# Output columns ordered for 512-byte stores, GpSimd's additions moved to VectorE, in an attention and gated-FFN kernel

## The chip, the core and the metric

The kernel runs on one core of one Trainium2 chip. The metric is the device time of one execution in microseconds; a kernel's time is the median of its runs.

## The reference, cut to what matters

```python
# x: 8 batches, 8 heads, 512 tokens, 64 wide; state: 32 rows a head; all float32
scores  = x @ state.T / 8;  xread = softmax(scores) @ state
scores2 = state @ x.T / 8;  sread = softmax(scores2) @ x
x = concat([xread, sread]) as 4352 rows of 512
x = ((x @ w1) * (x @ w2)) @ w3 @ w_out                      # 512 -> 1024 -> 1024 -> 512
return (sigmoid(x @ w_gate) * (x @ w_val)) @ w_out2         # 512 -> 1536 -> 512
```

The weights of both feed-forward parts arrive as 64-bit floats and are turned into 32-bit ones in the kernel.

## The kernel before

Every product is made of three passes of TensorE over a high and a low part of each operand (`split`: ScalarE copies the high part, a subtraction makes the low part).

**First half.** It does the attention and the first feed-forward part, one batch after another, with attention folded in between the products. Each batch is a loop over eight column blocks (`j`) and then four output blocks (`d`): twelve slots, in which other work is placed. The result `y` goes to DRAM (`y_d`), already transposed. In the same slots the weights of the second part are prepared: `prep_group` makes 18 groups of four steps (two loads with conversion, `sums`, `last`). A group holds the seven combinations of a 2 x 2 blocked weight that Winograd's form of Strassen's algorithm needs: three blocks as they are, and four sums (`sm`). All seven are split into the staging tile `wst`, the arithmetic on GpSimd, and one store on GpSimd's queue brings them to `w_d` or `wo_d`.

**Second half.** The 34 blocks of 128 token rows go in five pairs of 8, 8, 6, 6 and 6 blocks. One operand of a product is half a pair, 512 or 384 columns. Each pair takes three passes over 512 of the 1536 hidden columns. A pass is `gate_val` twice (14 steps each) and `down` (14 steps); a step is six products into one PSUM bank. `down` of a pass runs behind the first three steps of the next pass's `gate_val`. Its results are added up over the passes in eight SBUF tiles `acc[d, cc]` (`d`: 128 output columns, `cc`: half of the pair). Results that go into two tiles are copied to SBUF by ScalarE (`sv`) and added by GpSimd (`also`); the others are added by VectorE from PSUM (`more`).

The order of ScalarE, VectorE, GpSimd and SyncE is written out by hand: `later(k, cost, fn)` puts `fn` at the beginning of the k-th step from now, `begin` advances a model clock, and `fill` places parts of the next pair's `y` (`next_tokens`) where the model sees VectorE free. An operation of n columns counts n/720 us in it.

Weights stream through SyncE's queue (`Stream`): `wt`, one tile of 256 KB a step of `gate_val`, 19 tiles; `wo`, one of 512 KB for two steps of `down`, 4 tiles. A new load is issued behind the step that used the tile and waits for it in the queue. At the end of a pair, `store` transposes one `acc` tile in 32 x 32 blocks on VectorE into a tile `sv` (three of them, shared with `also`) and issues 16 or 12 stores of 32 partitions on the same queue, each 128 descriptors of 128 bytes:

```python
            for i, fn in enumerate(done):
                later(2 + 2 * i, n / 720, fn)
```

The last pair does the same behind the last product (`tail`). In the rows, the products of `gate_val` are L1386 and those of `down` L1543; the weight loads are L1246, the output stores L1480, their transposes L1466, `more` L1490, `also` L1494, subtractions of the second half (`minus`) L1109 and of the first (`split`) L163, and all copies of ScalarE L158.

Of the kernel before, what the change touches and what calls it, by code (L numbers as in the profile page):

```python
# [117 lines left out]
def tile_state_attention__then__gated_ffns(  # L118
# [19 lines left out]
    nc = tc.nc  # L138
# [124 lines left out]
    with tc.manual_schedule(engines={mybir.EngineType.PE}):  # L263
# [781 lines left out]
        def prep_group(dst, srcs, by_rows):  # L1045
# [6 lines left out]

            def sums():
                t = ab["t"] = p2["wst"].tile([P, 7, 2, 256], F32R, name="wst")
                sm = ab["sm"] = p2["wst"].tile([P, 4, 256], F32, name="sm")
                halves = [[v[:, i * 256 : (i + 1) * 256] for i in range(2)] for v in m]
                (a11, a12), (a21, a22) = halves if by_rows else zip(*halves)
                for o, x0, x1, op in (
                    (0, a21, a22, ALU.add),
                    (1, sm[:, 0], a11, ALU.subtract),  # L1060
                    (2, a11, a21, ALU.subtract),
                    (3, a12, sm[:, 1], ALU.subtract),
                ):
                    nc.gpsimd.tensor_tensor(out=sm[:, o], in0=x0, in1=x1, op=op)
                if by_rows:
                    split(
                        t[:, 0:2, 0], t[:, 0:2, 1], m[0].rearrange("p (k f) -> p k f", k=2),
                        sub=nc.gpsimd,
                    )
                else:  # L1070
                    split(t[:, 0, 0], t[:, 0, 1], a11, sub=nc.gpsimd)
                    split(t[:, 1, 0], t[:, 1, 1], a12, sub=nc.gpsimd)
                split(t[:, 2, 0], t[:, 2, 1], a22, sub=nc.gpsimd)

            def last():
                t = ab["t"]
                split(t[:, 3:7, 0], t[:, 3:7, 1], ab["sm"], sub=nc.gpsimd)
                nc.gpsimd.dma_start(out=dst, in_=t.rearrange("p o i f -> p (o i f)").bitcast(F32))
# [21 lines left out]
        def y_raw(c, kb, h, pool, w, queue=nc.sync):  # L1100
            n = blocks[c] * P // 2
            r = pool.tile([P, 2, w], F32, tag="raw", name="yf", bufs=3)
            queue.dma_start(
# [25 lines left out]
        for t, b in enumerate(order):  # L1129
# [124 lines left out]
        def next_tokens(c, at):  # L1254
# [9 lines left out]
            def get(kb, h, queue=nc.sync):  # L1264
                raw[kb, h] = y_raw(c, kb, h, c2, NB, queue)
                clock["load"] = landed[kb, h] = max(clock["load"], clock["us"] + 2.5) + 2.2

            def diffs(kb):
                (b11, b12), (b21, b22) = raw[kb, 0], raw[kb, 1]
                t[kb] = [c2.tile([P, NB], F32, tag="m", name="yt", bufs=3)[:, :n] for _ in range(3)]  # L1270
# [8 lines left out]
            def part(o, kb):  # L1279
                def fn():  # L1280
# [9 lines left out]
                    later(1, n / 720, lambda: (minus(y[1], v, y[0].bitcast(F32)), ready.add((c, o, kb))))  # L1290
                    if (o, kb) == (5, 0):
                        later(2, 0.0, lambda: get(1, 1, nc.scalar))
# [21 lines left out]
            out += [(at(9), False, lambda i=i: diff(1, i)) for i in range(4)]  # L1314
# [15 lines left out]
        def operand(s, jj):  # L1330
# [15 lines left out]
            later(1, n / 720, low)  # L1346
# [5 lines left out]
        def have(q, jj, cc, n):  # L1352

            cost = n / 720
# [18 lines left out]
        def gate_val(c, g, q, between):  # L1373
# [31 lines left out]
            def finish(a, jj, cc, o, what):  # L1405

                if a == 0:
# [6 lines left out]
                    vector(n / 720)  # L1414
# [225 lines left out]
```

## Time and profile before

| | |
|---|---|
| median of 3 runs | 1543.65 us (1542.5 to 1547.69) |
| the profiled execution | 1541.75 us, span 1540.0 us |
| granted clock of TensorE, mean | 0.937 of full speed |
| busy: TensorE, VectorE, ScalarE, GpSimd | 1318.2, 928.4, 661.6, 263.8 us |
| moved by DMA | 312.90 MB, 203 GB/s over the span |
| DMA packets under 512 bytes | 121552 of 240444 |

The span runs from the first to the last instruction; the time has 1.75 us more around it. Busy times of engines overlap, so they don't add up to the span.

### The profile page before, as it was taken

How to read it: one execution, taken by the hardware profiler on the slowest of the kernel's cores; microseconds unless marked ns; L12 is line 12 of the kernel's file. 1: busy time of each engine (PE TensorE's matmuls, PEld its weight loads, DVE VectorE, ACT ScalarE, POOL GpSimd, SP SyncE). 2: the span in 40 equal slices, each digit the busy share in tenths (PEclk: the TensorE clock that was granted, in tenths of full speed). 3: DMA queues.
4: the chain of work that ended last, by engine and by line, in shares of the span. 5: the costliest groups of instructions: out<-in, count | busy, mean ns of one | idle time of the engine just before them, and what ended most of it. 6: DMA issues, size and time to landing. Idle time of an engine off the chain costs nothing. (4 is left out here: it accounts for less than half of the span.)

```text
span 1540.0 us, 21873 instructions
## 1 busy us (share of the span) xinstructions
PE 1318.2 (86%) x7792; PEld 1120.7 (73%) x7792; DVE 928.4 (60%) x1532; ACT 661.6 (43%) x1274; POOL 263.8 (17%) x232
## 2 busy tenths in 40 slices
PE   8999999999999999999856999657996699876970
PEld 5587787777777798877745887557986699776970
DVE  5975766755777626577644569343683466753670
ACT  6964664665566534335212435131342243331330
POOL 0000452443354100030100032000210010100210
PEclk9999999999999999999978999887997899988995
DMA  8974776857866338676436776438874688548712
GB/s 300 336 211 151 230 262 240 277 218 272 296 224 234 143 115 311 199 228 200 128 87 196 203 215 181 116 85 278 262 221 126 191 274 259 163 111 265 235 49 34
DMA packets 240444, 312.90 MB, mean 203 GB/s; under 512 B 121552, under 2 KB 139472, under 8 KB 233424
## 3 DMA queue, kind: packets, MB, share of 16 engines
q1 hardware_dynamic: 229904, 263.54, 55.6%
q0 software_dynamic: 3168, 37.23, 6.4%
q10 hardware_dynamic: 7264, 10.75, 2.0%
q8 instruction: 62, 1.02, 0.3%
q14 instruction: 46, 0.38, 0.1%
HBM read 256.38 MB, written 55.05 MB: 202 GB/s over the span
## 5 line engine op out<-in xcount | busy, mean ns | idle before, releaser
L1386 PE MATMUL psA<-y,wt 128*128 128x384 f32 (+1 forms) x1440 | 311.4, 364 | 46.9 <-ACT u L158 45.1
L1543 PE MATMUL po<-ph,wo 128*128 128x384 f32 (+1 forms) x1260 | 265.6, 369 | 81.5 <-DMA wo<-wod 60.9
L1386 PEld LDWEIGHTS psA<-y,wt 128*128 128x128 f32 x1440 | 265.6, 193 | 74.9 <-ACT u L158 47.9
L1543 PEld LDWEIGHTS po<-ph,wo 128*128 128x128 f32 x1260 | 232.9, 195 | 111.8 <-issue 63.7
L158 ACT ACTIVATE u<-psA 128x384 f32<-128x384 f32 (+1 forms) x120 | 63.9, 532 | 300.0 <-PE psA L1386 265.8
L1494 POOL TENSOR_TENSOR acc<-sv,acc 128x384 f32<-128x384 f32 (+1 forms) x60 | 94.2, 1604 | 509.2 <-ACT sv L158 427.3
L1386 PE MATMUL psB<-y,wt 128*128 128x384 f32 (+1 forms) x720 | 163.1, 362 | 0.0
L1386 PEld LDWEIGHTS psB<-y,wt 128*128 128x128 f32 x720 | 133.2, 192 | 11.6
L1490 DVE TENSOR_TENSOR acc<-po,acc 128x384 f32<-128x384 f32 (+1 forms) x140 | 82.8, 601 | 91.5 <-PE po L1543 91.0
L225 PE MATMUL py<-u,wp 128*128 128x512 f32 (+1 forms) x576 | 133.0, 382 | 1.9 <-ACT u L158 1.1
L225 PE MATMUL pab<-aT,sw 128*128 128x512 f32 x448 | 124.0, 398 | 4.9 <-DVE asb L983 3.5
L225 PEld LDWEIGHTS py<-u,wp 128*128 128x128 f32 x576 | 102.9, 188 | 30.6 <-issue 7.5
L1386 PE MATMUL psC<-y,wt 128*128 128x384 f32 (+1 forms) x360 | 84.8, 372 | 26.1 <-DVE s L1419 26.1
L1109 DVE TENSOR_TENSOR ph<-p,ph 128x384 fp32r<-128x384 f32 (+1 forms) x120 | 96.0, 803 | 17.8 <-ACT ph L158 17.7
L1466 DVE STREAM_TRANSPOSE sv<-acc 128x384 f32<-128x384 f32 (+1 forms) x40 | 25.1, 628 | 128.9 <-DMA out<-sv 128.8
L225 PEld LDWEIGHTS pab<-aT,sw 128*128 128x128 f32 x448 | 82.6, 190 | 24.8 <-DVE asb L983 5.2
L163 DVE TENSOR_TENSOR u<-asb,u 128x512 fp32r<-128x512 f32 (+1 forms) x64 | 67.0, 1046 | 42.6 <-ACT u L158 42.3
L1386 PEld LDWEIGHTS psC<-y,wt 128*128 128x128 f32 x360 | 67.7, 197 | 34.3 <-DVE s L1419 28.6
L1415 ACT ACTIVATE p<-p 128x384 f32<-128x384 f32 (+1 forms) x90 | 50.7, 563 | 91.1 <-DVE p L1413 91.1
L158 ACT ACTIVATE ph<-t 128x384 fp32r<-128x384 f32 (+1 forms) x90 | 49.7, 563 | 75.2 <-DVE t L1109 74.1
L1413 DVE TENSOR_TENSOR p<-psB,u 128x384 f32<-128x384 f32 (+1 forms) x60 | 36.5, 609 | 73.0 <-ACT u L158 67.2
L158 ACT ACTIVATE ph<-p 128x384 fp32r<-128x384 f32 (+1 forms) x120 | 64.7, 561 | 28.6 <-DVE p L1422 28.5
(137 smaller groups left out, 1988.0 us busy)
## 6 DMA issues: line engine op xcount, KB each, us to landing
wt<-wd SPq DMA_DIRECT2D x420, 256.0 KB, 3.1
wo<-wod SPq DMA_DIRECT2D x105, 512.0 KB, 4.2
wq<-w12d SPq DMA_DIRECT2D x32, 1024.0 KB, 7.1
wd<-wst POOLq DMA_DIRECT2D x12, 1792.0 KB, 7.2
raw<-in_moe_w SPq DMA_DIRECT2D x32, 512.0 KB, 6.2
wod<-wst POOLq DMA_DIRECT2D x6, 1792.0 KB, 7.5
raw<-in_moe_w_out SPq DMA_DIRECT2D x20, 512.0 KB, 6.4
out<-sv SPq DMA_DIRECT2D x544, 16.0 KB, 1.5
```

Of the source, the lines that this page charges most:

```text
L158: return nc.scalar.activation(out=o, in_=i, func=AF.Copy)
L163: (sub or nc.vector).tensor_tensor(out=lo, in0=src, in1=hi.bitcast(F32), op=ALU.subtract)
L225: nc.tensor.matmul(o, w[i], xx[k], start=begin and n == 0 and i + k == 0, stop=False)
L1109: nc.vector.tensor_tensor(out=o, in0=x0, in1=x1, op=ALU.subtract)
L1386: nc.tensor.matmul(o, w[:, i, kb * P : (kb + 1) * P], xx[kb][h], start=start, stop=i == 1 and kb == 1, skip_group_check=True,)
L1413: nc.vector.tensor_tensor(out=t, in0=o, in1=kept[a, what], op=ALU.add)
L1415: later(2, 0.0, lambda: nc.scalar.activation(out=t, in_=t, func=AF.Sigmoid))
L1466: nc.vector.transpose(out=t, in_=acc[d, cc])
L1490: nc.vector.tensor_tensor(out=acc[d, cc], in0=o, in1=acc[d, cc], op=ALU.add)
L1494: nc.gpsimd.tensor_tensor(out=acc[d, cc], in0=v, in1=acc[d, cc], op=ALU.add)
L1543: nc.tensor.matmul(o, w[:, jj, i, d * P : (d + 1) * P], x[h], start=k in (1, 6, 2) and jj == 0 and i + h == 0, stop=jj == 1 and i == 1, sk ...
```

## The change

The columns of `w_out2` are taken in another order when its blocks are formed, so that a 32 x 32 transpose of the four `acc` tiles of one 128-row block leaves 128 neighbouring output columns beside each other. `store` then handles one block of 128 rows with all 512 columns: four transposes and four stores whose descriptors are 512 bytes. They are placed every three steps. For the last pair `last_store` turns a block with four transposes on TensorE into PSUM, ScalarE or VectorE copies it, and one store of 128 rows goes out, in turn on SyncE's and ScalarE's queue. The additions that GpSimd made in `also`, in the copy of `acc` and in `prep_group` are VectorE's; `wst` becomes two tiles of three and four blocks, each with a store of its own. The `y` of the next pair is loaded by four loads at once, its differences are formed as soon as they have landed, and it has 4 and 6 tiles (`raw`, `yt`) instead of 3 and 3; `wt` has 16 tiles instead of 19. The preparation uses twelve slots of a batch instead of eleven. The model counts n/840 instead of n/720 (these lines and a dropped argument `queue` are left out below).

```diff
+            def shape(v):
+                return v if by_rows else v.rearrange("p (c i d) -> p c i d", c=2, i=4)
             def sums():
-                t = ab["t"] = p2["wst"].tile([P, 7, 2, 256], F32R, name="wst")
                 sm = ab["sm"] = p2["wst"].tile([P, 4, 256], F32, name="sm")
-                halves = [[v[:, i * 256 : (i + 1) * 256] for i in range(2)] for v in m]
-                (a11, a12), (a21, a22) = halves if by_rows else zip(*halves)
+                t = p2["wst"].tile([P, 3, 2, 256], F32R, name="wsta")
+                if by_rows:
+                    (a11, a12), (a21, a22) = [[v[:, i * 256 : (i + 1) * 256] for i in range(2)] for v in m]
+                else:
+                    (a11, a21), (a12, a22) = [
+                        [
+                            v.rearrange("p (i c d) -> p c i d", i=4, c=4)[:, 2 * i : 2 * i + 2]
+                            for i in range(2)
+                        ]
+                        for v in m
+                    ]
+                s1, s2, s3, s4 = (shape(sm[:, o]) for o in range(4))
                 for o, x0, x1, op in (
-                    (0, a21, a22, ALU.add),
-                    (1, sm[:, 0], a11, ALU.subtract),
-                    (2, a11, a21, ALU.subtract),
-                    (3, a12, sm[:, 1], ALU.subtract),
+                    (s1, a21, a22, ALU.add),
+                    (s2, s1, a11, ALU.subtract),
+                    (s3, a11, a21, ALU.subtract),
+                    (s4, a12, s2, ALU.subtract),
                 ):
-                    nc.gpsimd.tensor_tensor(out=sm[:, o], in0=x0, in1=x1, op=op)
-                if by_rows:
-                    split(
-                        t[:, 0:2, 0], t[:, 0:2, 1], m[0].rearrange("p (k f) -> p k f", k=2),
-                        sub=nc.gpsimd,
-                    )
-                else:
-                    split(t[:, 0, 0], t[:, 0, 1], a11, sub=nc.gpsimd)
-                    split(t[:, 1, 0], t[:, 1, 1], a12, sub=nc.gpsimd)
-                split(t[:, 2, 0], t[:, 2, 1], a22, sub=nc.gpsimd)
+                    nc.vector.tensor_tensor(out=o, in0=x0, in1=x1, op=op)
+                for o, v in enumerate((a11, a12, a22)):
+                    split(shape(t[:, o, 0]), shape(t[:, o, 1]), v)
+                store(0, t)
             def last():
-                t = ab["t"]
-                split(t[:, 3:7, 0], t[:, 3:7, 1], ab["sm"], sub=nc.gpsimd)
-                nc.gpsimd.dma_start(out=dst, in_=t.rearrange("p o i f -> p (o i f)").bitcast(F32))
+                t = p2["wst"].tile([P, 4, 2, 256], F32R, name="wstb")
+                for o in range(0, 4, 2):
+                    split(t[:, o : o + 2, 0], t[:, o : o + 2, 1], ab["sm"][:, o : o + 2])
+                store(3, t)
+            def store(o, t):
+                n = t.shape[1]
+                nc.gpsimd.dma_start(
+                    out=dst[:, o * 512 : (o + n) * 512],
+                    in_=t.rearrange("p o i f -> p (o i f)").bitcast(F32),
+                )
...
-                for i in range(t == 1, 11) if t + 1 < B else range(JF):
+                for i in range(t == 1, JF + KM):
...
-            get(0, 0)
-            if clock["now"] == 0:
-                get(0, 1)
-                get(1, 0)
-                first = [at(1)] * 3
-                out = []
-            else:
-                first = [here((0, 0)), here((0, 0), (0, 1)), here((1, 0))]
-                out = [(lambda: True, None, lambda k=k: get(*k)) for k in ((0, 1), (1, 0))]
-            out += [(first[0], True, part(0, 0))]
-            out += [(first[1], False, lambda i=i: diff(0, i)) for i in range(4)]
+            for k in ((0, 0), (0, 1), (1, 0), (1, 1)):
+                get(*k)
+            out = []
+            for kb in range(2):
+                out += [(here((kb, 0), (kb, 1)), False, lambda i=i, kb=kb: diff(kb, i)) for i in range(4)]
+            out += [(at(1), True, part(0, 0))]
...
-            out += [(at(9), False, lambda i=i: diff(1, i)) for i in range(4)]
...
-        def store(c, d, cc, n):
-            t = c2.tile([P, NB], F32, name="sv", bufs=3)[:, :n]
-            nc.vector.transpose(out=t, in_=acc[d, cc])
+        def rows(c, cc, m):
+            blk = first[c] + (cc * blocks[c] // 2) + m
+            if blk < B * SC:
+                b, r = order[blk // SC], blk % SC
+                return out[b * ROWS : b * ROWS + S].rearrange("(j t c) e -> c t j e", c=SC, t=32)[r]
+            b = 4 * (blk - B * SC)
+            return out.rearrange("(b r) e -> r b e", b=B)[S:, b : b + 4]
+        def store(c, cc, m):
+            t = c2.tile([P, 4, KM, 32], F32, name="sv", bufs=3)
+            for d in range(KM):
+                nc.vector.transpose(out=t[:, :, d], in_=acc[d, cc][:, m * P : (m + 1) * P])
             def out_():
-                for m in range(n // P):
-                    blk = first[c] + cc * (n // P) + m
-                    if blk < B * SC:
-                        b, r = order[blk // SC], blk % SC
-                        dst = out[b * ROWS : b * ROWS + S].rearrange("(j t c) e -> c t j e", c=SC, t=32)[r]
-                    else:
-                        b = 4 * (blk - B * SC)
-                        dst = out.rearrange("(b r) e -> r b e", b=B)[S:, b : b + 4]
-                    dst = dst[:, :, d * P : (d + 1) * P].rearrange("t j (i d) -> i t j d", d=32)
-                    for i in range(4):
-                        src = t[32 * i : 32 * i + 32, m * P : (m + 1) * P]
-                        nc.sync.dma_start(out=dst[i], in_=src.rearrange("t (j d) -> t j d", d=32))
+                dst = rows(c, cc, m)
+                for i in range(4):
+                    nc.sync.dma_start(
+                        out=dst[:, :, i * P : (i + 1) * P],
+                        in_=t[32 * i : 32 * i + 32].rearrange("t j d e -> t j (d e)"),
+                    )
             later(2, 0.0, out_)
+        def last_store(c, cc, m, i):
+            pt = ps2.tile([P, DM], F32, tag="A", name="pot", bufs=2)
+            for d in range(KM):
+                nc.tensor.transpose(pt[:, d * P : (d + 1) * P], acc[d, cc][:, m * P : (m + 1) * P], unit)
+            t = c2.tile([P, 4, KM, 32], F32, name="sv", bufs=3)
+            copy("dve" if i % 2 else "act", t, pt.rearrange("p (c i d) -> p i c d", c=KM, i=4))
+            blk = first[c] + (cc * blocks[c] // 2) + m
+            if blk < B * SC:
+                b, r = order[blk // SC], blk % SC
+                dst = out[b * ROWS : b * ROWS + S].rearrange("(p c) e -> c p e", c=SC)[r]
+            else:
+                b = 4 * (blk - B * SC)
+                dst = out.rearrange("(b r) e -> b r e", b=B)[b : b + 4, S:]
+            (nc.scalar if i % 2 else nc.sync).dma_start(out=dst, in_=t.rearrange("p i c d -> p (i c d)"))
...
-                nc.gpsimd.tensor_tensor(out=acc[d, cc], in0=v, in1=acc[d, cc], op=ALU.add)
+                nc.vector.tensor_tensor(out=acc[d, cc], in0=v, in1=acc[d, cc], op=ALU.add)
...
-                        nc.gpsimd.tensor_copy(out=new_acc(2 + d, 0), in_=s)
+                        later(1, n / 1600, lambda: nc.vector.tensor_copy(out=new_acc(2 + d, 0), in_=s))
                     else:
                         s = c2.tile([P, NB], F32, name="sv", bufs=3)[:, :n]
                         copy("act", s, o)
-                        also(s, d, 0)
-                        also(s, 2 + d, 0)
+                        later(1, n / 840, lambda: also(s, d, 0))
+                        later(2, n / 840, lambda: also(s, 2 + d, 0))
                 elif k == 5:
                     if g == 0:
                         copy("act", new_acc(2 + d, 1), o)
                     else:
                         s = c2.tile([P, NB], F32, name="sv", bufs=3)[:, :n]
                         copy("act", s, o)
-                        also(s, 2 + d, 1)
+                        later(2, n / 840, lambda: also(s, 2 + d, 1))
                 elif k == 6:
                     if g == 0:
...
-                    if g == NPASS - 1:
-                        if tail:
-                            later(1, n / 720, lambda: store(c, *e, n))
-                        else:
-                            done.append(lambda: store(c, *e, n))
...
-            for i, fn in enumerate(done):
-                later(2 + 2 * i, n / 720, fn)
+            if g == NPASS - 1:
+                todo = [(cc, m) for cc in (1, 0) for m in range(n // P)]
+                for i, (cc, m) in enumerate(todo):
+                    if tail:
+                        last_store(c, cc, m, i)
+                    else:
+                        later(2 + 3 * i, 1.0, lambda cc=cc, m=m: store(c, cc, m))
...
-        names += [("t0", 1, NB), ("t1", 1, NB), ("sv", 3, NB), ("yt", 3, NB), ("u4", 1, NB)]
+        names += [("t0", 1, NB), ("t1", 1, NB), ("sv", 3, NB), ("yt", 6, NB), ("u4", 1, NB)]
...
+        unit = c2.tile([P, P], F32, name="unit")
+        make_identity(nc, unit)
...
-            "wt", [P, 2, 256], 19,
+            "wt", [P, 2, 256], 16,
```

## Rows read from the trace of the kernel before

**Rows 1.** Page, first part: busy time, share of the span, instructions.
```profile
PE 1318.2 (86%) x7792; PEld 1120.7 (73%) x7792; DVE 928.4 (60%) x1532; ACT 661.6 (43%) x1274; POOL 263.8 (17%) x232
```

**Rows 2.** Timeline of TensorE: start, length, line, tiles, shape, merged count.
```profile
609.00 19.20 PE L1543 MATMUL po<-ph,wo 128*128 128x512 f32 x84
628.04 2.88 PE L1386 MATMUL psA<-y,wt 128*128 128x512 f32 x12
...
1436.80 14.72 PE L1543 MATMUL po<-ph,wo 128*128 128x384 f32 x84
1451.36 2.24 PE L1386 MATMUL psA<-y,wt 128*128 128x384 f32 x12
```

**Rows 3.** Windows over the changes of pair and the tail: length, busy PE, PEld, DVE, ACT, POOL, clock, DMA.
```profile
725.76:884.42 158.66, 124.04 (x506) 99.72 (x504) 84.57 (x123) 49.30 (x89) 12.19 (x8) 0.89 0.55 153
941.44:1088.30 146.86, 100.25 (x506) 94.12 (x506) 70.81 (x120) 40.29 (x88) 12.26 (x8) 0.85 0.57 165
1137.01:1263.07 126.06, 94.91 (x506) 92.38 (x505) 65.74 (x122) 39.58 (x89) 9.81 (x8) 0.88 0.63 187
1311.13:1436.80 125.67, 95.22 (x505) 92.69 (x505) 65.73 (x122) 39.56 (x89) 9.80 (x8) 0.88 0.63 186
1496.50:1540.00 43.50, 0.00 (x0) 0.00 (x0) 4.66 (x9) 0.00 (x0) 0.00 (x0) 0.53 0.24 34
```

**Rows 4.** Timeline of SyncE's queue: a change of pair, and the end.
```profile
1165.71 0.85 SPq L1246 DMA_DIRECT2D wt<-wd  x2
1166.65 5.60 SPq L1480 DMA_DIRECT2D out<-sv  x12
...
1492.19 45.72 SPq L1480 DMA_DIRECT2D out<-sv  x96
```

**Rows 5.** TensorE's waits: engine, tile, line, releaser: total us, times, longest.
```profile
PE po L1543 <- DMA wo<-wod: 60.9, 4, 19.5
...
PE po L1543 <- DVE acc L1490: 14.5, 7, 2.6
...
PE po L1543 <- ACT sv L158: 4.9, 10, 0.8
```

**Rows 6.** Tile `sv`: idle time before its instructions, its stores' landing.
```profile
  DMA out<-sv: 128.8, 25
...
DMA to landing us min/median/max: 1.4/1.5/4.0
```

**Rows 7.** Timelines of VectorE and GpSimd in `down` of pass 1 or 2.
```profile
747.53 1.29 DVE L1109 TENSOR_TENSOR y<-yt,y 128x512 fp32r<-128x512 f32 x2
...
1143.81 1.36 DVE L1109 TENSOR_TENSOR t<-p,t 128x384 f32<-128x384 f32 x1
...
1152.81 1.47 DVE L1490 TENSOR_TENSOR acc<-po,acc 128x384 f32<-128x384 f32 x3
...
1155.14 1.00 DVE L1490 TENSOR_TENSOR acc<-po,acc 128x384 f32<-128x384 f32 x2
...
1139.87 7.46 POOL L1494 TENSOR_TENSOR acc<-sv,acc 128x384 f32<-128x384 f32 x6 [41.28 <-DVE ph L1109]
```

**Rows 8.** A window at full pace with 384 columns.
```profile
1233.00:1263.00 30.00, 30.00 (x175) 30.00 (x174) 16.64 (x32) 11.84 (x26) 0.00 (x0) 1.00 0.83 260
```

**Rows 9.** Window over the first half, batches 1 to 7 (columns as rows 3).
```profile
115.50:577.50 462.00, 446.23 (x3409) 357.27 (x3407) 297.45 (x454) 263.58 (x489) 154.05 (x151) 0.99 0.64 222
```

**Rows 10.** Timelines of the first half: TensorE, ScalarE, VectorE.
```profile
279.28 0.65 PE L290 MATMUL pxt<-ident,xn 128*128 128x128 f32 x4 [2.96 <-ACT xT L158]
...
274.52 0.94 ACT L158 ACTIVATE wst<-m 128x512 fp32r<-128x512 f32 x2 [2.67 <-DMA wod<-wst]
...
542.30 0.42 DVE L163 TENSOR_TENSOR u<-asb,u 128x256 fp32r<-128x256 f32 x1
```

**Rows 11.** Groups by line and shape: busy us, mean ns, idle before.
```profile
L163 DVE TENSOR_TENSOR u<-asb,u 128x512 fp32r<-128x512 f32 x56 | 63.6, 1135 | 40.7 <-ACT u L158 40.3
```

**Rows 12.** View of DMA issues, KB each, median us to landing.
```profile
yd<-ysb ACTq DMA_DIRECT2D x28, 256.0 KB, 3.1
```

More of the change, by code (lines that the diff above doesn't have):

```diff
@@ L1098, in y_tiles, with y_raw @@
             return [p2["c1"].tile([P, NB], F32R, name=f"y{i}", bufs=16 - i)[:, :n] for i in range(2)]
-        def y_raw(c, kb, h, pool, w, queue=nc.sync):
+        def y_raw(c, kb, h, pool, w, bufs=3):
             n = blocks[c] * P // 2
-            r = pool.tile([P, 2, w], F32, tag="raw", name="yf", bufs=3)
-            queue.dma_start(
+            r = pool.tile([P, 2, w], F32, tag="raw", name="yf", bufs=bufs)
+            nc.sync.dma_start(
                 out=r[:, :, :n], in_=y_d[c][2 * h + kb].rearrange("p (c n) -> p c n", c=2)
@@ L1262, in next_tokens, with get @@
             landed = {}
-            def get(kb, h, queue=nc.sync):
-                raw[kb, h] = y_raw(c, kb, h, c2, NB, queue)
+            def get(kb, h):
+                raw[kb, h] = y_raw(c, kb, h, c2, NB, 4)
                 clock["load"] = landed[kb, h] = max(clock["load"], clock["us"] + 2.5) + 2.2
@@ L1269, in diffs @@
                 (b11, b12), (b21, b22) = raw[kb, 0], raw[kb, 1]
-                t[kb] = [c2.tile([P, NB], F32, tag="m", name="yt", bufs=3)[:, :n] for _ in range(3)]
+                t[kb] = [c2.tile([P, NB], F32, tag="m", name="yt", bufs=6)[:, :n] for _ in range(3)]
                 t1, t2, t3 = t[kb]
@@ L1289, in fn @@
                     copy("act", y[0], v)
-                    later(1, n / 720, lambda: (minus(y[1], v, y[0].bitcast(F32)), ready.add((c, o, kb))))
-                    if (o, kb) == (5, 0):
-                        later(2, 0.0, lambda: get(1, 1, nc.scalar))
+                    later(1, n / 840, lambda: (minus(y[1], v, y[0].bitcast(F32)), ready.add((c, o, kb))))
                 return fn
@@ L1344, in low @@
                 parts[s, jj] = hi, lo
-            later(1, n / 720, low)
+            later(1, n / 840, low)
         def first_sum(jj, n):
@@ L1352, in have @@
         def have(q, jj, cc, n):
-            cost = n / 720
+            cost = n / 840
             if q == 0:
@@ L1413, in finish @@
                     nc.vector.tensor_tensor(out=t, in0=o, in1=kept[a, what], op=ALU.add)
-                    vector(n / 720)
+                    vector(n / 840)
                     later(2, 0.0, lambda: nc.scalar.activation(out=t, in_=t, func=AF.Sigmoid))
@@ L1419, in finish @@
                     nc.vector.tensor_tensor(out=kept[a, what], in0=o, in1=kept[a, what], op=ALU.add)
-                    vector(n / 720)
+                    vector(n / 840)
                     o = kept[a, what]
                 nc.vector.tensor_tensor(out=t, in0=o, in1=t, op=ALU.mult)
-                vector(n / 720)
+                vector(n / 840)
                 have(q, jj, cc, n)
@@ new lines, in store @@
+        def store(c, cc, m):
+            t = c2.tile([P, 4, KM, 32], F32, name="sv", bufs=3)
+            for d in range(KM):
+                nc.vector.transpose(out=t[:, :, d], in_=acc[d, cc][:, m * P : (m + 1) * P])
+            def out_():
+                dst = rows(c, cc, m)
+                for i in range(4):
+                    nc.sync.dma_start(
+                        out=dst[:, :, i * P : (i + 1) * P],
+                        in_=t[32 * i : 32 * i + 32].rearrange("t j d e -> t j (d e)"),
+                    )
+            later(2, 0.0, out_)
@@ L1486, in down @@
             banks = {}
-            done = []
             def more(o, d, cc):
                 nc.vector.tensor_tensor(out=acc[d, cc], in0=o, in1=acc[d, cc], op=ALU.add)
-                vector(n / 720)
+                vector(n / 840)
             def also(v, d, cc):
-                nc.gpsimd.tensor_tensor(out=acc[d, cc], in0=v, in1=acc[d, cc], op=ALU.add)
+                nc.vector.tensor_tensor(out=acc[d, cc], in0=v, in1=acc[d, cc], op=ALU.add)
             def new_acc(d, cc):
```

## The prediction

> **What bounds the kernel now.** Start with the busy shares: TensorE is at 86%, VectorE at 60%, the others lower [rows 1], so the time should be TensorE's work plus the places where it stands. The timeline of TensorE gives the work. A full `down` of 84 products takes 19.04 us from its first product to the next stage's at 512 columns, and 14.56 us at 384 [rows 2]; a `down` has 14 steps of six products, so a step is 1.36 us or 1.04 us. The second half of the program has 252 steps at 512 columns (two pairs, three passes, 42 steps) and 378 at 384. At 609.00, when the first `down` starts [rows 2], 31 of the 512 ones are done. What is left is 221 x 1.36 + 378 x 1.04 = 693.7 us, so without any stall TensorE would end at 1302.7. It ends at 1496.5, and the span at 1540 [rows 3]. So 193.8 us are stall or slow clock, and 43.5 us are a tail without TensorE.
>
> Next, the windows between one `down` and the second after it, over each change of pair [rows 3]. They last 158.66, 146.86, 126.06 and 125.67 us; their steps need 114.24 (84 x 1.36), 91.84 (14 x 1.36 + 70 x 1.04), 87.36 and 87.36 (84 x 1.04). The surplus is 44.4 + 55.0 + 38.7 + 38.3 = 176.4 us of the 193.8. [...]
>
> The queue of SyncE tells why [rows 4]. The output stores of the finished pair go into the same queue as the weights, twelve (384 columns) in 5.6 us, then only two `wt` loads, then twelve again; eight such groups. TensorE eats a `wt` tile a step and gets two in about 6.6 us. Behind them stand the `wo` loads, the largest wait of TensorE by name (60.9 us, four times) [rows 5]. VectorE stands too: its transposes wait 128.8 us, 25 times, for a staging tile `sv` to be stored [rows 6], and the gate's sums queue behind them. The same queue makes the tail: 96 stores in 45.7 us, 0.476 us each, though each lands 1.5 us after its issue [rows 4, 6].
>
> **The stores.** A 16 KB store and a 256 KB `wt` load both hold the queue about 0.45 us [rows 4], so I price an issue, not its bytes. The change packs four stores into one of 64 KB: a pair of eight blocks issues 32 instead of 128, one of six 24 instead of 96. In three steps (3.1 or 4.1 us) the queue now gets four stores (1.9 us) and three `wt` loads (1.4 us): 3.3 us for 3.1 at 384 columns, six times over, a lag of 1.2 us against a lead of 16 tiles or 16.6 us. Three tiles of lead are lost (19 to 16), 3.1 us that nothing then needs. From below the starvation goes wholly; from above the new stores cost the transfer engines more than I think (next). I take it as gone.
>
> **The transfer engines.** With TensorE at full pace at 384 columns they are 0.83 busy at 260 GB/s [rows 8]: 0.051 us per KB and engine, 105 ns a 2 KB packet. The tail moves 34 GB/s of 128-byte packets at 0.24 [rows 3]: 14 ns each. On the line between them 512 bytes cost 32 ns, four times the 128-byte price 58 ns. Six blocks are 3072 packets: 6 us of all sixteen engines, at most 11, in a pass of 43.7 us that is busy for 35 to 36. That is 0.95 to nearly 1.1 in such a pass. The tiles of lead absorb most; I take 5 us of stall in all, 0 to 25 as bounds.
>
> **GpSimd's additions on VectorE, second half.** While GpSimd does its six additions (7.46 us), a VectorE subtraction takes 1.36 us; unhindered, three last 1.47 and two 1.00, so they follow each other in 0.47 us at 384 columns, and one lasts 0.53; at 512 the step is 0.61 [rows 7] (1.29 less the 0.68 of one). With an operation let through for each of GpSimd's, VectorE loses 7.46 - 6 x 0.47 = 4.6 us in each `down` of passes 1 and 2, and pays 2.8 us when it adds itself: 1.8 us better, more at 512. The waits of TensorE for `acc` (14.5 us, seven times, at most 2.6) [rows 5] are of that size; I leave 4 us. The moved additions wait for ScalarE's copy, with the gate's sums queued behind them, but they are placed one or two steps (1.04 to 2.7 us) after it: zero, if ScalarE keeps up. The waits for the copies `sv` (4.9 us) stay. Two copies a pair also move; at the subtraction's price they are 2 x 0.61 us, under a `down` of 14 us or more.
>
> Transposes become four times as many, 128 wide. By the code a pass gives VectorE 58 operations (20 sums and products of the gate, 8 sums of operands, 14 low parts, 10 `more`, 6 `also`) and 22 more with the next pair's `y` (14 low parts, 8 differences): 80 x 0.47 = 38 us of 43.7 at most; the pass that stores needs 58 x 0.47 + 24 x about 0.25 (estimate: a quarter of 0.47 to all of it) = 33. That cover is thin where work bunches: I keep 4 us of the waits seen there, and up to 30 if VectorE falls behind. [...] No row shows a 128-wide transpose.
>
> Together TensorE's loss falls from 193.8 us to 5 + 4 + 5 + 4 = 18: **-175.8 us**.
>
> **The four loads of `y`** now go out together on SyncE when pass 2 begins: 1.5 MB, 6 us at 260 GB/s, under the same lead. VectorE's differences come earlier and spread; zero.
>
> **The first half.** TensorE stands about 16 us of 462 [rows 9]. Some of it is GpSimd's: ScalarE waited 2.67 us for the one staging tile still being stored, and TensorE then 2.96 us for ScalarE's `xT` [rows 10]. Two tiles, each used again four slots later, remove that. VectorE takes on seven 256-wide operations (0.42 us [rows 10]) and two 512-wide ones (0.61 [rows 7]) a group, 4.2 us, 18 groups: 75 us. It gets back at least 56 x (1.135 - 0.68) = 25 us of one line, with 1.29 - 0.61 = 0.68 for an unhindered one [rows 7, 11]. Its 297 us of 462 become about 347, 75%; a step j of 2.72 us (twelve products at the 0.227 of [rows 2]) has 1.2 us of VectorE's own work, to which the additions bring 1.05 on average (4.2 over four slots) beside the conversions that already run there. It just fits. GpSimd issues two stores a group instead of one, on a queue that is otherwise idle then: zero. The steps left for the last batch fall from seven to one. I take **-6 us**, from -14 to +10.
>
> **The tail.** After the last product: cc = 1 blocks are complete, so the first is transposed (0.65 us [rows 10]), copied (about as long), stored (256 KB, 3.1 us from issue to landing [rows 12]). There are three `sv` tiles, so blocks 4 to 6 wait for those landings: 0.65 + 0.65 + 0.4 + 3.1 = 4.8 us, the third of them at about 6, then 0.7 + 3.5: **10.5 us** (8 to 15) instead of 43.5, **-33 us**. Every second store goes by ScalarE's queue behind its copies, 0.45 us that the landings cover. [...]
>
> **Sum.** The profiled execution took 1541.75 us: 1541.75 - 175.8 - 6 - 33 = 1327. The median of the runs is 1.9 us above it, so **1329 us**.
>
> **Rivals.**
> Transfer engines bind (0.12): at the upper packet price the changes of pair keep 25 us, and `wo` again arrives last: about 1350. For it: 0.83 already. Against: the two pairs of 512 columns have a third more time.
> VectorE binds (0.14): all it takes on and does not get back, 50 us in the first half, 15 of transposes, lands on TensorE's path: 1329 + 65 = 1394; half of it is likelier, 1360. For it: 75% on average, bunched. Against: GpSimd's blocking goes.
> The stores run at a byte rate (0.03): 64 KB at the tail's 34 GB/s is 1.9 us, then nothing is gained from packing, only the 6 us: about 1535. Against: `wt` loads of 256 KB issue as fast.
> Slower (0.02): VectorE, in order, waits for `sv`. A store needs the tile of the third store before, issued seven steps earlier (7.3 us at 384 columns). Thirty stores in threes, each three losing (landing - 7.3 us): the gain of 215 us is gone from a landing of 29 us on; at 32 us the time is 1329 + 10 x 24.7 = 1576. Landings so far are 4.0 us at most [rows 6].
>
> **The numbers.** Forecast 0.69, own range 1312 to 1345. Range: the low end takes the loss at 12 us (-6), the first half at -14 (-8) and the tail at 8 (-2.5), 1312; the high end 1372 holds the transfer rival and most of VectorE's. Outside lie about 0.08 below and 0.12 above. A change of under 0.3% (5 us) can't be told from none here. Faster 0.96, same 0.02 (part of the byte-rate case), slower 0.02.
>
> **What would show it.** Stores in fours of about 1.9 us with three `wt` loads between; the windows over the changes of pair at about 116, 94, 90 and 90 us with the clock near 1.0; no idle VectorE for `out<-sv`; no GpSimd arithmetic in the second half and subtractions never above 0.7 us; a last matrix product near 1315 and 10 us behind it. Wrong if `wo` is still awaited over changes of pair, if TensorE's waits for VectorE grow past 30 us, or if the first half ends later than 609 + 10.

## The result and the profile after

The changed kernel takes **1316.63 us** (median of 4 runs, 1314.77 to 1318.98). The kernel before, run beside it, takes 1545.67, so the ratio is 0.8519 with a 95% interval of 0.8494 to 0.8544. The forecast was 1329 us, the stated range 1312 to 1372. The profiled execution took 1318.98 us, its span is 1317.2.

The page's busy line of the changed kernel, to be held against [rows 1]:

```profile
PE 1277.9 (97%) x7816; PEld 1103.7 (84%) x7816; DVE 950.4 (72%) x1839; ACT 672.3 (51%) x1307; POOL 24.9 (2%) x50
```

TensorE went from 86% to 97%. The same bookkeeping as in the prediction: the first `down` starts at 582.63 (before 609.00 [rows 2]); 693.7 us of steps later it would be 1276.3; the last product ends at 1299.4; the span ends at 1317.2. So the first half gave 26.4 us, the second half loses 23.1 instead of 193.8, and the tail is 17.8 instead of 43.5. The windows over the changes of pair and the tail, columns as in [rows 3]:

```profile
696.87:811.60 114.73, 114.56 (x506) 94.49 (x504) 79.49 (x149) 46.33 (x84) 0.00 (x0) 1.00 0.74 213
867.78:968.20 100.42, 95.19 (x506) 91.28 (x505) 67.76 (x148) 38.32 (x84) 0.00 (x0) 0.97 0.79 241
1016.03:1106.81 90.78, 88.20 (x505) 87.26 (x505) 62.78 (x140) 37.54 (x85) 0.00 (x0) 1.00 0.85 260
1152.17:1242.47 90.30, 88.28 (x505) 87.23 (x505) 62.87 (x140) 37.53 (x85) 0.00 (x0) 1.00 0.85 262
1299.40:1317.20 17.80, 3.16 (x24) 2.29 (x22) 2.63 (x4) 1.79 (x3) 0.00 (x0) 0.65 0.32 89
```

The first four are the changes of pair, the last is the tail. The changes of pair but for the second are within 3.5 us of what their steps need (114.24, 91.84, 87.36, 87.36), and the granted clock in them is 0.97 to 1.00 where it was 0.85 to 0.89. The second, the only one well over (8.6 us), is the stretch in which the pair of eight blocks is stored while the next pair's steps are already 384 wide. SyncE's queue in it; TensorE's waits from 560 us on; and TensorE at the end of the longest of them:

```profile
910.54 1.79 SPq L1486 DMA_DIRECT2D out<-sv  x4
912.43 1.74 SPq L1260 DMA_DIRECT2D wt<-wd  x3
...
918.15 2.03 SPq L1486 DMA_DIRECT2D out<-sv  x4
920.29 2.89 SPq L1260 DMA_DIRECT2D wt<-wd  x4
923.26 2.26 SPq L1260 DMA_DIRECT2D wo<-wod  x4
```

```profile
PE po L1561 <- DMA wo<-wod: 11.2, 5, 5.2
PE po L1561 <- ACT sv L158: 3.4, 6, 0.9
PE pot L1496 <- ACT sv L158: 1.5, 2, 1.2
```

```profile
929.94 2.58 PE L1561 MATMUL po<-ph,wo 128*128 128x384 f32 x7 [5.23 <-DMA wo<-wod]
```

Stores in fours of 1.8 to 2.0 us with three loads between are what the prediction described. But from 902 to 923 us the queue has 36 issues end to end, and the `wo` load behind them leaves at 923.26, though the pass's first `down` began at 916.22 and frees a tile every 2.08 us (two steps of 1.04; 105 tiles for 15 `down`s of 14 steps): about 5 us late, and the longest wait is 5.2. The load is then used 6.7 us after its issue, where loads of `wo` land in 4.0 us in the median, so it landed slowly too. The waits for `wo` and `sv` in the list are 14.6 of the 23.1 us. The rest has no name in it; a part is slow clock, 0.72 from 924.7 to 935 us, behind the longest wait. `acc` is awaited no more (14.5 us before [rows 5]). Instructions on the staging tile `sv`, and three groups of VectorE:

```profile
L1481 DVE STREAM_TRANSPOSE sv<-acc x112: 267/270/314, 717.2 to 1186.3; 128x128 f32<-128x128 f32 x112
...
DVE sv L1481: 1.6, 3
...
DMA to landing us min/median/max: 2.0/3.7/7.6
```

```profile
L163 DVE TENSOR_TENSOR u<-asb,u 128x512 fp32r<-128x512 f32 x56 | 38.5, 687 | 3.2 <-ACT u L158 2.9
L1481 DVE STREAM_TRANSPOSE sv<-acc 128x128 f32<-128x128 f32 x112 | 24.7, 278 | 1.6 <-DMA out<-sv 1.6
L1517 DVE TENSOR_TENSOR acc<-sv,acc 128x384 f32<-128x384 f32 x36 | 18.8, 551 | 0.0
```

VectorE's transposes wait 1.6 us for a stored tile instead of 128.8 [rows 6]. The first group fell from 1135 to 687 ns an operation [rows 11].

### The profile page after: what moved, and what is told of

Same layout as the page of the kernel before. It is cut to its first block, busy times and chain, and to the rows that moved or that the text cites. A ratio compares the mean times of both kernels' runs of the same rounds, so it can differ in the third digit from the quotient of the medians.

```text
span 1317.2 us, 21517 instructions
## 1 busy us (share of the span) xinstructions
PE 1277.9 (97%) x7816; PEld 1103.7 (84%) x7816; DVE 950.4 (72%) x1839; ACT 672.3 (51%) x1307; POOL 24.9 (2%) x50
## 2 busy tenths in 40 slices
DMA packets 181666, 312.86 MB, mean 238 GB/s; under 512 B 45368, under 2 KB 77624, under 8 KB 174648
## 4 chain that ended last, share of the span: by engine, by line
PE 84%; DMA 6%; DVE 5%; ACT 3%; issue 1%; SPq 0%; DVEq 0%; ACTq 0%
PE psA L1392 20%; PE po L1561 16%; PE psB L1392 10%; PE pab L225 9%; PE py L225 8%; PE psC L1392 5%; PE pab L228 4%; PE py L228 4%; DMA wo<-wod 3%; PE pwp L225 2%; PE psw L533 2%; DMA wq<-w12d 2%; PE pwp L228 1%; PE pxt L290 1%; DVE y L1123 1%; DMA out<-sv 1%
## 5 line engine op out<-in xcount | busy, mean ns | idle before, releaser
L1392 PE MATMUL psA<-y,wt 128*128 128x384 f32 (+1 forms) x1440 | 299.8, 356 | 0.0
L1392 PEld LDWEIGHTS psA<-y,wt 128*128 128x128 f32 x1440 | 258.9, 188 | 22.5
L1561 PE MATMUL po<-ph,wo 128*128 128x384 f32 (+1 forms) x1260 | 256.0, 362 | 14.6 <-DMA wo<-wod 11.2
L1561 PEld LDWEIGHTS po<-ph,wo 128*128 128x128 f32 x1260 | 229.5, 191 | 38.7 <-issue 8.3
L1392 PE MATMUL psB<-y,wt 128*128 128x384 f32 (+1 forms) x720 | 159.5, 356 | 0.0
L1392 PEld LDWEIGHTS psB<-y,wt 128*128 128x128 f32 x720 | 130.0, 188 | 11.2
L225 PE MATMUL py<-u,wp 128*128 128x512 f32 (+1 forms) x576 | 131.8, 381 | 0.0
L225 PE MATMUL pab<-aT,sw 128*128 128x512 f32 x448 | 122.1, 394 | 0.8 <-DVE aT L163 0.8
L1123 DVE TENSOR_TENSOR ph<-p,ph 128x384 fp32r<-128x384 f32 (+1 forms) x120 | 72.5, 605 | 10.4 <-ACT ph L158 10.4
L1392 PE MATMUL psC<-y,wt 128*128 128x384 f32 (+1 forms) x360 | 79.8, 356 | 0.0
L228 PE MATMUL pab<-aT,sw 128*128 128x512 f32 x224 | 69.1, 390 | 0.0
L228 PE MATMUL py<-u,wp 128*128 128x512 f32 (+1 forms) x288 | 67.7, 377 | 0.0
L1123 DVE TENSOR_TENSOR ph<-t,ph 128x384 fp32r<-128x384 f32 (+1 forms) x90 | 54.1, 604 | 10.8 <-ACT ph L158 10.8
```

The costliest lines, as they stand in the source:

```text
L225: nc.tensor.matmul(o, w[i], xx[k], start=begin and n == 0 and i + k == 0, stop=False)
L228: nc.tensor.matmul(o, w[1 - late], xx[late], start=False, stop=end and n == len(pairs) - 1)
L1123: nc.vector.tensor_tensor(out=o, in0=x0, in1=x1, op=ALU.subtract)
L1392: nc.tensor.matmul(o, w[:, i, kb * P : (kb + 1) * P], xx[kb][h], start=start, stop=i == 1 and kb == 1, skip_group_check=True,)
L1561: nc.tensor.matmul(o, w[:, jj, i, d * P : (d + 1) * P], x[h], start=k in (1, 6, 2) and jj == 0 and i + h == 0, stop=jj == 1 and i == 1, sk ...
```

## The experiments

All are edits of the changed kernel. "Loss" is the time from the first `down` to the last product less 693.7 us (after: 23.1); a tail runs from there to the end of the span. Both are read from one profiled execution of each kernel, and so is the first `down`. How far these differ without an edit that bears on them can be read from the kernels below: with the first half unchanged, the first `down` starts between 581.78 and 585.45 us; with the second half unchanged, the loss is 20.3 to 24.1 us; with the last stores unchanged, the tail is 16.5 to 17.8 us.

**1. The stores cut into sixteen issues a block again, with 512-byte packets kept.** Is it the issues or the small packets?

```diff
-                    nc.sync.dma_start(out=dst[:, :, i * P : (i + 1) * P], ...)
+                    for j in range(4):
+                        nc.sync.dma_start(out=dst[:, j, i * P : (i + 1) * P], ...)
```

> The changed kernel with each 64 KB store of a finished block cut into four of 16 KB: 16 issues a block as before, the same bytes in the same 512-byte descriptors; the last pair's stores as in the changed kernel. Theory: the queue's issues make the stall; 16 x 0.45 = 7.2 us of queue for three steps (3.1 or 4.1 us), so the changes of pair get most of the 176 us back that they lost before: 1430 to 1490. Rival: the small descriptors made it; then it stays within 6 us of 1316.6.

1459.23 us (ratio 0.9457, 0.9432 to 0.9482). SyncE's queue and TensorE's waits in it:

```profile
777.48 7.37 SPq L1487 DMA_DIRECT2D out<-sv  x16
784.94 1.32 SPq L1260 DMA_DIRECT2D wt<-wd  x3
```

```profile
PE po L1562 <- DMA wo<-wod: 76.3, 6, 21.4
PE psA L1392 <- ACT u L158: 33.7, 8, 6.8
```

A 16 KB issue costs 0.46 us (7.37 / 16), a 64 KB one 0.45 (1.79 / 4). The stall comes back with the data in the same 512-byte packets (the profile page's packets under 512 bytes rise by 5376, from 45368 to 50744: sixteen for each of the 336 further issues). The loss is 161.9 us. The number of issues was the cause of 142.6 us of the 229.0; the rival falls. What 128-byte packets in few issues would cost, no run shows.

**2. The `also` additions and `acc` copies back on GpSimd**, issued at once as before.

```diff
-                nc.vector.tensor_tensor(out=acc[d, cc], in0=v, in1=acc[d, cc], op=ALU.add)
+                nc.gpsimd.tensor_tensor(out=acc[d, cc], in0=v, in1=acc[d, cc], op=ALU.add)
...
```

> The changed kernel (1316.6 us) with the six additions of `down` and the copies of `acc` back on GpSimd. Theory: GpSimd's additions hold VectorE's subtractions up (1.36 us instead of 0.55 while they run), so each `down` of passes 1 and 2 loses more on VectorE than it saves; TensorE's waits for `acc`, 0 now, come back to about 10 us and the time to 1324 to 1336. Rival: the additions load VectorE and nothing else, so the time falls to 1305 to 1316.

1343.29 us (0.87, 0.8678 to 0.8723): +26.7, more than either theory's figure. The loss is 49.0. Waits of TensorE; then the timeline of GpSimd's six additions in one `down` and of VectorE beside them:

```profile
PE po L1561 <- DVE acc L1513: 20.4, 11, 3.1
PE po L1561 <- DMA wo<-wod: 6.4, 2, 4.9
```

```profile
986.15 8.43 POOL L1517 TENSOR_TENSOR acc<-sv,acc 128x384 f32<-128x384 f32 x6 [48.95 <-ACT sv L158]
...
988.50 1.37 DVE L1123 TENSOR_TENSOR yt<-yf 128x384 f32<-128x384 f32 x1
989.91 1.26 DVE L1123 TENSOR_TENSOR yt<-yf,yt 128x384 f32<-128x384 f32 x1
```

Beside GpSimd a subtraction takes 1.3 us in place of 0.55. The loss grows by 26 us, which do not all stand in one wait: `acc` shows 20.4 of them.

**3. The weight preparation.** Four kernels: its arithmetic on GpSimd with both staging tiles; one staging tile of seven blocks with the arithmetic on VectorE; both; both and the slots of before. The cuts show, in this order, one line of the arithmetic, of the staging tile and of the slots.

```diff
-                    nc.vector.tensor_tensor(out=o, in0=x0, in1=x1, op=op)
+                    nc.gpsimd.tensor_tensor(out=o, in0=x0, in1=x1, op=op)
...
-                t = p2["wst"].tile([P, 3, 2, 256], F32R, name="wsta")
+                t = ab["t"] = p2["wst"].tile([P, 7, 2, 256], F32R, name="wst")
...
-                for i in range(t == 1, JF + KM):
+                for i in range(t == 1, 11) if t + 1 < B else range(JF):
```

> The changed kernel with the sums and subtractions of the weight preparation back on GpSimd, both staging tiles kept. In the changed kernel the first `down` starts at 582.6 us, 26.4 earlier than before. Theory A: GpSimd's arithmetic, by holding VectorE up, made those 26 us; the first `down` comes 13 to 24 us later and the time is 1329 to 1341. Theory B: the single staging tile made them, ScalarE waiting for its store; then the first `down` comes 0 to 6 us later and the time is 1316 to 1323.

> The changed kernel with one staging tile of seven blocks and one store a group, the arithmetic on VectorE. Theory A (GpSimd's arithmetic made the 26 us of the first half): the first `down` comes 0 to 5 us later, 1316 to 1322. Theory B (the single tile made them): 10 to 24 us later, 1327 to 1341.

> Both edits of the weight preparation undone together: the sums and subtractions on GpSimd and one staging tile of seven blocks in place of two. Singly they moved the first down product by 10.7 us and 3.2 us; the whole change moved it by 26.4 us. Theory A (the two hold each other up: with one staging tile the next group's arithmetic waits for the store, and GpSimd's longer arithmetic makes that wait longer): first down at 601 to 609 us, 1336 to 1345 us. Theory B (the two are independent, and the rest of the 26.4 us came from spreading the preparation over more slots of a batch): first down at 595 to 599 us, 1328 to 1334 us.

> As the kernel with both preparation edits undone, and its steps put back into the slots of before (the first 11 of a batch, in the last batch all of the w1 steps, in place of all w1 and w2 steps). Theory A (GpSimd and staging tile alone): within 3 us of the kernel without the slots' edit. Theory B (slots carry the rest): 8 to 14 us later than it, with the first down at 605 to 611 us; TensorE's wait for the transposed x (7.3 us before) back at 5 us or more.

| kernel | us (ratio, interval) | first `down` | `u<-asb,u`, ns |
|---|---|---|---|
| after | 1316.63 | 582.63 | 687 |
| arithmetic on GpSimd | 1329.14 (0.8608, 0.8582 to 0.8634) | 593.29 | 952 |
| one staging tile | 1320.84 (0.8553, 0.8522 to 0.8585) | 585.83 | 686 |
| both | 1340.82 (0.8678, 0.8658 to 0.8697) | 606.20 | 1104 |
| both and the slots | 1340.94 (0.8685, 0.8661 to 0.8709) | 605.38 | 1097 |
| before | 1545.67 | 609.00 | 1135 |

ScalarE's wait for a staging tile with one tile and VectorE's arithmetic, and in the kernel with both; then the additions `u<-asb,u` with the arithmetic on GpSimd:

```profile
ACT wst L158 <- DMA wd<-wst: 3.0, 3, 1.6
```

```profile
ACT wst L158 <- DMA wd<-wst: 24.7, 9, 4.2
```

```profile
L163 DVE TENSOR_TENSOR u<-asb,u 128x512 fp32r<-128x512 f32 x56 | 53.3, 952 | 28.9 <-ACT u L158 28.6
```

The first `down` comes 10.7 us later with the arithmetic on GpSimd, 3.2 later with one staging tile (barely more than unchanged first halves differ by, and its time is not clear of the changed kernel's), and 23.6 later with both. So neither edit alone made the 26.4 us; the two hold each other up. The waits of ScalarE for the tile (24.7 us against 3.0) fit the reason that slower arithmetic delays the store that the only tile waits for. So theory A of the third kernel holds, and in the fourth the slots give nothing that shows. The first kernel's `down` lies just under its theory A, its time at the edge of it; the second kernel is as its theory A has it. `u<-asb,u` is lengthened by GpSimd's arithmetic alone: it takes 686 and 687 ns without that arithmetic, 952 to 1135 with it.

**4. What the 11.2 us of `wo` waits are: transfer engines or queue.** The other blocks' stores on ScalarE's queue (112 of 28 blocks; the expectation's 120 and the prediction's "thirty stores" count two blocks too many); and five `wo` tiles with 14 `wt` tiles.

```diff
-                    nc.sync.dma_start(
+                    nc.scalar.dma_start(
```

```diff
-            "wt", [P, 2, 256], 16,
+            "wt", [P, 2, 256], 14,
...
-            "wo", [P, 2, 2, 256], 4,
+            "wo", [P, 2, 2, 256], 5,
```

> The 120 stores of the other 30 blocks are issued by ScalarE in place of SyncE. Theory A: the 11.2 us that TensorE waits for w_out2 tiles come from the transfer engines (their share stood at 0.93 to 1.05 in the stretches where it waited), so they stay at 8 to 14 us; ScalarE loses 120 issues of about 0.45 us, 54 us in 700 in which it has room: 1314 to 1322 us. Theory B: the loads stand behind the stores in SyncE's queue; then the waits for w_out2 fall under 4 us: 1307 to 1312 us.

> Five w_out2 tiles in place of four, paid for by 14 in place of 16 w_gate/w_val tiles. Theory A: the wait of 5.2 us at the change from the pair of 8 blocks to the next is a lead that runs out, so one more tile of lead (one step, 3.8 us at 512 columns and less at 384) takes about 4 us of it: waits for w_out2 at 4 to 7 us, 1311 to 1316 us. Theory B: the transfer engines owe the same bytes whatever the lead: waits for w_out2 stay near 11 us or pass to wt (gate waits), 1315 to 1322 us.

Stores on ScalarE: 1326.19 us (0.858, 0.8556 to 0.8604), loss 27.1. Its waits, a window in it at the place of the 5.2 us wait, and ScalarE there:

```profile
PE psA L1392 <- ACT s L158: 7.5, 5, 2.5
...
PE po L1561 <- DMA wo<-wod: 1.3, 1, 1.3
```

```profile
916.00:930.00 14.00, 13.12 (x76) 12.73 (x75) 11.53 (x27) 7.12 (x18) 0.00 (x0) 1.00 0.88 260
```

```profile
916.92 5.64 ACTq L1486 DMA_DIRECT2D out<-sv  x7
922.60 0.53 ACT L1421 ACTIVATE p<-p 128x384 f32<-128x384 f32 x1 [6.41 <-DMA out<-sv]
```

The waits for `wo` are all but gone while the transfer engines are still 0.88 busy (0.93 in the same window of the changed kernel): the loads stood behind the stores in SyncE's queue. On ScalarE the same stores hold up its copies instead, and the kernel is 9.6 us slower by the medians, 4.6 by the profiled executions. So the waits follow theory B, the time neither theory. How much of the 11.2 us was the load's slow landing, and not its late issue, no run separates.

Five tiles: 1307.14 us (0.8454, 0.8432 to 0.8475), loss 10.9:

```profile
PE po L1561 <- DMA wo<-wod: 2.1, 1, 2.1
```

A tile more is 2.1 to 2.7 us of lead (the expectation's 3.8 was wrong); the waits fall by 9.1 us over five places, and two tiles fewer of `wt` cost nothing that shows. That is better than theory A had it; theory B falls.

**5. The tail.** Of the six last stores (the expectations say four), the second and third hold state rows, and these two have the batch, four steps, as the output's outermost dimension. One kernel cuts each into four transfers; one gives every last store a tile of its own.

```diff
-            (nc.scalar if i % 2 else nc.sync).dma_start(out=dst, in_=t.rearrange("p i c d -> p (i c d)"))
...
+            if blk < B * SC:
+                queue.dma_start(out=dst, in_=v)
+            else:
+                for k in range(4):
+                    queue.dma_start(out=dst[k], in_=v[32 * k : 32 * k + 32])
```

```diff
-            t = c2.tile([P, 4, KM, 32], F32, name="sv", bufs=3)
+            t = c2.tile([P, 4, KM, 32], F32, tag="m", name="yt", bufs=6)
```

> The four last stores of the tail each write 128 rows of 2 KB. Two of them (the extra rows past S) have the batch as the outermost dimension of the output, four steps of it; here each of these two is four transfers of 32 rows, one a batch. Theory A: such a store keeps only a few transfer engines busy, which is why its landing took 9.9 us against 1.4 to 3.1 us for stores in this trace that are spread; then the wait of VectorE's copy for the staging tile (9.5 us) goes, and the tail from the last product to the end falls from 17.8 to 9 to 12 us: 1308 to 1311 us. Theory B: the landing is slow because the stores meet each other and the last loads, so that the shape does not matter: tail 16 to 19 us, 1315 to 1319 us, and the three more issues cost up to 1.5 us.

> Only the staging of the four last stores changes: each has a tile of its own in place of three that take turns. Theory A (few transfer engines a store): the wait for the staging tile goes, but the stores of the extra rows still take about 10 us to land, so the end is set by the last of them: tail 13 to 16 us, 1312 to 1315 us. Theory B (the turn of the staging tiles alone makes the tail long): tail 8 to 11 us, 1307 to 1310 us.

VectorE's last two copies and the piece of the chain before the second in the changed kernel; then VectorE's last copy with the cut stores:

```profile
1302.67 0.69 DVE L159 COPY sv<-pot 128x512 f32<-128x512 f32 x1 [1.70 <-DMA out<-sv]
1312.90 0.69 DVE L159 COPY sv<-pot 128x512 f32<-128x512 f32 x1 [9.54 <-DMA out<-sv]
```

```profile
1302.88 9.91 DMA out<-sv
```

```profile
1306.57 0.69 DVE L159 COPY sv<-pot 128x512 f32<-128x512 f32 x1 [2.52 <-DMA out<-sv]
```

The last copy waits 9.5 us for the tile of the third store, which is issued at 1302.88 and lands 9.9 us later. Cut by batch: 1312.95 us (0.8484, 0.8461 to 0.8506), tail 10.9 as theory A has it; the time is 2 us above that theory's, and its interval overlaps the changed kernel's. A tile each: 1316.55 us (0.8514, 0.849 to 0.8538), tail 17.0: the wait for a tile is gone, but the end does not move, as the slow landings themselves set it (a little later even than theory A's 13 to 16). DMA issues on ScalarE's queue in the three kernels (after, cut, a tile each), KB and median us to landing:

```profile
out<-sv ACTq DMA_DIRECT2D x3, 256.0 KB, 4.8
```

```profile
out<-sv ACTq DMA_DIRECT2D x2, 256.0 KB, 2.2
out<-sv ACTq DMA_DIRECT2D x4, 64.0 KB, 1.8
```

```profile
out<-yt ACTq DMA_DIRECT2D x3, 256.0 KB, 6.9
```

The lines of 256 KB are medians of stores of other rows, 128 of them outermost, since the profile gives no landing for an uncut store of state rows: beside such a store the others land slowly as well (4.8 and 6.9 us, the slowest 7.6 and 10.6), beside cut ones in 2.2. The semaphore events in the traces tell the two kinds apart. Each of the other last stores, and each cut one, tells of its landing by sixteen events; an uncut store of state rows tells of it by four, behind one at its issue (the third store's at 1310.64, 1311.32, 1311.91 and 1312.78 us). The shape of the store is the cause: cut in four, the same rows land in 1.8 us in the median, and the tail falls from 17.8 to 10.9. By which means the shape does it was not shown; which engines a store used, no view here tells.

**6. Put together**: five `wo` tiles, cut stores, a tile each; and the same with the other blocks' stores on GpSimd's queue.

> Five w_out2 tiles with 14 w_gate/w_val tiles, the extra rows' last stores cut in four by batch, and a staging tile for each last store. If the three are independent: 1307 from the five tiles, less 4 to 7 for the cut stores, less 0 to 2.5 for the staging: 1298 to 1303 us, with a tail of 8.5 to 10 us. Rival: with no wait for staging all last stores leave within 5 us and their landing or their issues (ten of about 0.45 us on two queues) set the end: tail 10.5 to 13 us, 1303 to 1307 us.

> The kernel with five w_out2 tiles, cut last stores and a staging tile for each, with the stores of the other blocks on GpSimd's queue in place of SyncE's. GpSimd has no work in the second half any more. Theory A (SyncE's queue is what is left: TensorE loses 9.4 us between the first down and the last product, 2.7 of them in waits for w_out2): the loss falls to 5 to 7 us, 1295 to 1299 us. Theory B (GpSimd's issues are dearer than 0.45 us, or building their descriptors holds VectorE as its additions did, or the stores land later and VectorE's transposes wait for their tile): waits for acc or sv come up, 1302 to 1325 us.

The first takes 1300.19 us (0.8411, 0.8392 to 0.843), loss 9.4, tail 10.1, the time as expected of three independent gains; the second 1295.69 us (0.8385, 0.8363 to 0.8406), loss 7.3, tail 10.6. The page's busy line of the second and two views of it, the stores and TensorE's waits:

```profile
PE 1276.3 (98%) x7816; PEld 1102.9 (85%) x7816; DVE 949.7 (73%) x1839; ACT 672.5 (52%) x1307; POOL 86.4 (7%) x162
```

```profile
out<-sv POOLq DMA_DIRECT2D x112, 64.0 KB, 4.1
```

```profile
PE po L1567 <- ACT sv L158: 3.4, 6, 0.9
...
PE po L1567 <- DMA wo<-wod: 0.8, 1, 0.8
```

Theory B of the second falls, since no wait for `acc` or for a stored tile comes up. Theory A fits, but is not shown: the waits for `wo` fall from 2.7 to 0.8 us, while the gain over the first (0.3%, overlapping intervals) and the fall of the loss by 2.1 us are within what unchanged kernels differ by. Both beat the changed kernel, the second by 1.6% (0.8385 / 0.8519 = 0.984).

## Why the prediction was right, by its steps

The forecast named the cause and the size of the main gain, the stores. That the total came within 12.4 us is in part luck: the first half gave 20.4 us more than forecast, beyond its bounds, while the loss and the tail took 12.4 us back.

The experiments undo 142.6 us (issues), 26.7 (GpSimd's additions) and 24.2 (preparation), and the tail fell by 25.7: together 219 of the 229 us, if what was undone singly adds up. Medians are from different chips, on which the kernel before differs by up to 1.5 us, so the rest stays unassigned.

- **The stores** (starvation wholly gone): right in the main, by experiment 1. The windows came out at 114.73, 100.42, 90.78 and 90.30 for 116, 94, 90 and 90. It is not wholly gone: `wo` is still awaited over changes of pair, which the prediction had named as a sign of being wrong, for 11.2 us where it was 60.9.
- **The transfer engines** (5 us of stall): mis-sized and misplaced. The waits for `wo` are 11.2 us, and they come from SyncE's queue: four `wo` tiles of lead behind 36 issues (experiment 4). The prediction's "lead of 16 tiles" counted the `wt` tiles alone, and its remark that the 512-column pairs have more time passed over that the second pair of eight is stored in a pass of 384. Packets were priced a little high: in 43.7 us that hold all stores of a pair of six (from 1032 us) the transfer engines are 0.92 busy, where 0.95 to nearly 1.1 was forecast.
- **GpSimd's additions** (waits for `acc` from 14.5 to 4): the mechanism is right (beside them a subtraction takes 1.3 us in place of 0.55, experiment 2), the size too small. They are zero, and experiment 2 gives 26.7 us, where the step had left 10.5 of gain. The step itself worked out 1.8 us for each of ten `down`s, but took the smaller figure of the named waits.
- **Transposes and VectorE's load** (4 us): right, and no wait of TensorE in the second half names VectorE. One transpose takes 278 ns, and four in a row 0.88 us where one of 512 columns takes 0.69 to 0.71. So a wide transpose cut in four costs 0.17 to 0.19 us more.
- **The waits for `sv`** (5 us): 3.4.
- **The first half** (-6 us, from -14): the failed step, -26.4. It took TensorE's standing time, "about 16 us of 462", as the ceiling. Six whole batches, between the same products (x2535), of before and after:

```profile
171.42:504.50 333.08, 320.50 (x2535) 251.13 (x2534) 233.35 (x348) 202.73 (x376) 140.82 (x138) 0.99 0.73 255
```

```profile
168.83:482.83 314.00, 313.43 (x2535) 250.96 (x2534) 262.25 (x499) 211.20 (x400) 19.73 (x35) 1.00 0.79 274
```

Of 19.1 us, 12.0 were idle (12.6 to 0.6); 7.1 were counted as busy: the same products took longer. Another 2.6 and 4.7 us were gained ahead of and behind these batches. VectorE's load came as worked out: from 115.5 to 540 us it is busy for 324.03 of 424.50 us, 76% where 75% was forecast, and `u<-asb,u` shrank by the 0.45 us put down for it. What failed is the ceiling: the two edits together were worth 23.6 us of the first half (experiment 3), where the prediction allowed at most 14.
- **The tail** (43.5 to 10.5): mis-sized, 17.8. It priced every 256 KB store at 3.1 us [rows 12]; a store of state rows took 9.9, and others beside it up to 7.6. With these stores cut by batch the tail measures 10.9. TensorE's transposes were not priced too low: eight of them, two blocks, took 1.03 to 1.17 us, where the step had 0.65 for one block, and from 1300 to 1304 us the granted clock was 1.00.

Against the sum of 1327 the profiled execution is 8.0 us lower: first half -20.4, loss +5.1, tail +7.3. The median lies another 4.3 below that comparison, since it is 2.4 under its profiled execution where it was 1.9 above before.

## What to carry to other kernels

Count the issues in front of a load in its queue, in order, and compare them with the lead in tiles of that very load (36 issues against four `wo` tiles here): bytes and engine shares did not show it, with the transfer engines 0.93 busy where TensorE waited for `wo` and 0.88 with the stores on ScalarE's queue, where it hardly did. Idle time of the bound engine was a floor for what its stalls cost here, not a ceiling (12.0 us of idle time went, 19.1 us were gained); compare whole periods between the same instructions. Where a last store sets the end, look at its outermost dimension before counting its bytes (9.9 us for 256 KB here, 1.8 for its parts).

## What the runs showed of the hardware that was not expected

A 256 KB store with an outermost dimension of four landed in 9.9 us; cut in four, its parts of 64 KB landed in 1.8 us in the median on ScalarE's queue. Stores of 256 KB with 128 rows outermost took 2.1 to 2.2 beside cut ones and up to 10.6 beside uncut ones (a tile each). GpSimd issues a 64 KB store in 0.55 us (548 ns median), little dearer than SyncE's 0.45, and such stores held up no VectorE operation that TensorE waited for.
